# Low halves of the weights by one VectorE operation, the first casts of two items by ScalarE, and two units' scores as one TensorE task

## The chip, the cores and the metric

The kernel runs on one core of one Trainium2 chip. The metric is the device time of one execution in microseconds (us), as the median of repeated runs. Engines are named as in the profile: PE is TensorE, DVE is VectorE, ACT is ScalarE, POOL is GpSimd and SP is SyncE, whose queue issues most transfers. PEld is the loading of PE's stationary operand.

## What is computed

Block-sparse attention over 4 batches, 8 heads, 768 tokens and head size 64, followed by a two-layer network with a leaky ReLU. Everything is float32 at the interface, except that the weights of the network come as float64 in the arrays and the three random blocks of each query block as integers.

```python
scores = scale * np.matmul(q, k.transpose(0, 1, 3, 2))
# a query block of 32 sees: its neighbours (|i - j| <= 1), block 0, the last block,
# three sampled blocks; query blocks 0 and 23 see all
scores = np.where(mask, scores, -1000000000.0)
scores = scores - np.max(scores, axis=-1, keepdims=True)
attn = np.exp(scores)
attn = attn / (np.sum(attn, axis=-1, keepdims=True) + 1e-09)
x = np.matmul(attn, v)           # 3072 tokens of 512 after the heads are put side by side
h = x @ w_in                     # 512 x 2048
out = np.maximum(0.01 * h, h) @ w_out   # 2048 x 512
```

## The kernel before

**Two halves for each number.** PE multiplies float16. To keep the precision, every operand is scaled by a power of two and split into a high half, which is the value cast to float16, and a low half, which is the value minus its high half, again as float16. A product is made of three matmuls (high by high, high by low, low by high).

**Units and items.** The queries are cut in tiles T of two blocks (64 rows; tile 0 holds the first and the last block, which see all keys). A unit is one tile with one pair of heads hp; two units, hp and hp+1, make a pair. Four tiles with four head pairs each make an item of 16 units; there are 12 items, three to a batch, and so 192 units, numbered in u.n. In tiles other than 0 a unit's keys are 384: 6 fixed blocks and 6 sampled ones, which GpSimd copies out of the turned keys kt into the tile kg (line 1111) for all heads at once. Units of tile 0 have two parts of 384 keys.

**The way of a unit.** unit_scores (line 1165): four matmuls of 64 x 384 put the scores in one of the two PSUM banks s0 and s1; the left operands are half as wide as PE, and two such matmuls run side by side. unit_ttr (1189): DVE reads the scores, adds the mask em, writes p and the minimum mx. unit_exp (1200): ACT's exponential, with sums. pair_norm (1210): reciprocals r for both units of the pair. unit_high (1222): ACT makes the high half of p times r in pp. unit_split (1229): DVE makes the low half, and a transfer that transposes puts both in one of six tiles pt. pair_av (1245): twelve matmuls for each unit multiply pt with the gathered values vg into the bank av0. tile_evac (1263): ACT, DVE, ACT and POOL turn a finished tile of av0 into the two halves of x.

**The network.** For an item of 256 tokens, FF is worked off in 8 chunks. ffn_h (1285): 24 matmuls make a chunk of h in a PSUM bank. ffn_act1 (1298, ACT) and ffn_max (1303, DVE) make the leaky ReLU in ht. ffn_act2 (1308) casts it to the high half of g on DVE and subtracts on POOL for the low half. ffn_o (1313): 12 matmuls with the right-hand weights. For items 0 and 1 ("early": 2) the chunks become eligible quarter by quarter, as soon as that quarter's weights are made; later items need all of them. add_ffn (1422) queues an item's chunks "lead" (8) steps after its last unit, and refill (1434) releases them once its four tiles are evacuated (nx is 4).

**The weights.** w_in and w_out are cut in four quarters each, eight parts in the order wi0, wo0, wi1, ... wo3. Parts 0 to 5 are handled in two groups of 128 x 1024, parts 6 and 7 in four of 128 x 512. decode (813) turns the 64-bit patterns to float32 with one ACT and three DVE operations. squares (665) sums squares on PE for the scale. Then finish (864) splits each group, by the letter that "wsplit" has for the part. With "p" (parts 0 to 5 before):

```python
nc.scalar.activation(hi, g.d3, AF.Copy, scale=s[:, :1])
nc.scalar.activation(g.d, g.d, AF.Copy, scale=s[:, :1])
nc.gpsimd.tensor_tensor(out=lo, in0=g.d3, in1=hi, op=ALU.subtract)
```

With "d" (part 6 before) a single DVE scalar_tensor_tensor takes the place of the last two lines. Part 7 has a branch of its own, which is the same before and after.

**What sets the order.** The program text does not set it. Each call of an engine is recorded as a task with the memory cells that it reads and writes (class Plan, line 182; Engine, 433), and with a priority: plan.level (237) gives 1000 + 200 for each step, a step being one unit. plan.block (244) joins several PE matmuls into one task. Plan.trial (253) then plays the engines with a table of costs (466): each engine takes the ready task of lowest priority value, and PE adds a penalty (stay) for a task whose operands have another width than the last one's ("a" for half, "f" for full). Then the latest start of each task becomes its priority, and the trial is made again, up to four times, as long as the modelled end improves. The order of the best trial is issued, and each engine works through its own part of it in order.

The main loop (1575) goes through the units. In each step it takes the letters of "ord" in turn, "dtsixScmgovabphw". Those that matter here: d is pair_norm, t is unit_ttr, s is split_step, i is unit_high, x is unit_exp, S is the scores of the next unit, g is ffn_act2, a is av_step, v is one stage of tile_evac, h is ffn_h. split_step (1546) keeps count of the pt tiles in use (tlive) and calls av_step(True) where the next would exceed "pt" (6). When it has split the second unit of a pair, it puts the pair in pend_av, due "av_lag" (3) steps later; av_step (1557) takes due pairs out.

Of the kernel before, what the change touches and what calls it, by code (L numbers as in the profile page):

```python
# [34 lines left out]
    "bs": 1500,  # L35
    "kcopy": 330.0, "load": 800.0, "fetch": 1100.0, "early": 2,
    "pe_t": 16,
    "passes": 4,
    "stay_ns": 2000.0,
    "kg_dma": 0,  # L40
    "flag": 1,
    "g": 2,
    "g_at": 0,
# [20 lines left out]
    "wp": [2, 5, 14, 17, 20, 23, 26, 29],  # L64
    "wlead": 4,
    "wr": [(0, 1.0), (4, 3.0), (10, 4.0), (18, 4.5)],
    "wsplit": "ppppppdd",
    "xbufs": 3,
}

# [111 lines left out]
class Plan:  # L182
# [59 lines left out]

    @contextmanager
    def block(self, eng="PE"):
        g = Task()
        g.eng, g.run, g.busy, g.late, g.kind, g.loads, g.reads, g.writes = eng, [], 0.0, 0.0, "", [], set(), set()
        g.port = False
        self.group = g
        yield
        self.group = None  # L250
        self.add(g)
# [214 lines left out]
def cost(eng, method, a, k):  # L466

    out = k.get("out", a[0] if a else None)
    n = elements(out)
    apply = lambda x: hasattr(x, "ap")  # L470
    if eng == "PE":
        lhs, rhs = a[1], a[2]
        cols = elements(rhs)
        if lhs.dtype == F32:
            return 60.0 + 4 * cols, 300.0 + 4 * cols, "f", []
        half = elements(lhs) <= 64
        t = cols / 2.4 + 2.5
        return (t / 2 if half else t), t + 180, ("a" if half else "f"), []
    if eng == "SP" or method.startswith("dma"):
        turned = method == "dma_start_transpose"  # L480
        w = transfer(k["out"], k["in_"], turned)
        rows = len([d for d in list(k["out"].ap) if d[1] > 1])
        busy = 1050.0 + 0.37 * n if turned else 425.0 + 110 * max(0, rows - 1)
        return busy, busy, "", [w]
    if eng == "DVE":
        ptr = sum(1 for x in (k.get("scalar"), k.get("scalar1"), k.get("scale")) if apply(x)) > 0
        src = [x for m, x in k.items() if m in ("in0", "in1", "in_") and apply(x)]
        wide = [x for x in src if elements(x) > 1]
        f = 1.0
        if method in ("tensor_copy", "tensor_scalar") and len(wide) == 1 and wide[0].space == bass.MemoryType.SB:  # L490
            f = 0.5
            if method == "tensor_copy" and wide[0].dtype == F16 and out.dtype == F16:
                f = 0.25
        if method == "tensor_reduce":
            n = elements(k["in_"])
        d = 145 + 62 * ptr + n * f / 0.96
        if len(wide) == 2 and all(x.space == bass.MemoryType.SB for x in wide) and n >= 256:
            d *= 1.08
        acc = method == "tensor_tensor_reduce"
        return max(d - 70, 60.0), d + 12 + 80 * acc, "", []  # L500
    if eng == "ACT":
# [10 lines left out]
def tile_block_sparse_attention_ffn(  # L512
# [67 lines left out]
    cst, pw, sm, pa, pf = Pool(1), Pool(1), Pool(4), Pool(2), Pool(2)  # L580
    banks = [Buffer(psum.tile([P, 512], F32, name=n)) for n in ("s0", "s1", "o0", "o1", "h0", "h1", "h2", "av0")]
    group = {"s": banks[:2], "o": banks[2:4], "h": banks[4:7], "av": banks[7:]}
    turn = dict.fromkeys(group, 0)
    wide = Buffer(banks[0].ap[:, KEYS:])
    slots = [Buffer(banks[1].ap[:, at:at + 16]) for at in range(KEYS, 512, 16)]
# [102 lines left out]
    eq = tmps[:NB, 150:150 + NR * NB].rearrange("p (r b) -> p r b", r=NR)  # L688
    sels = [tmps[:NB, 222 + P * a:222 + P * (a + 1)].rearrange("p (a b c) -> p a b c", a=2, b=2) for a in range(2)]
    assert 222 + 2 * P <= DM and 6 + 2 * NB * NR <= 150  # L690
    offs = cst.tile([1, NT - 1, 8], I32, name="offs")
    vrow = cst.tile([P, 2, NT - 1], I32, name="vrow")
    lane = cst.tile([P, 2, NT - 1], I32, name="lane")
    mask = cst.tile([P, NT - 1, SLOTS], F32, name="mask")
    lane_m = cst.tile([P, NT - 1, SLOTS], F32, name="maskhalf")

    def load_constants():
        nc.sync.dma_start(out=eye, in_=c_eye)
# [101 lines left out]
    def load_w(g):  # L800
# [12 lines left out]
        def decode():  # L813


            plan.prio = 1000.0 + 200 * CFG["wp"][g.part]
            lo, hi, f, d = raw[:, :, 0], raw[:, :, 1], g.d, g.d.bitcast(I32)
            nc.scalar.activation(f, hi.bitcast(F32), AF.Copy, scale=2.0 ** -112)
            nc.vector.tensor_scalar(out=d, in0=d, scalar1=3, scalar2=None, op0=ALU.logical_shift_left)
            nc.vector.scalar_tensor_tensor(  # L820
                out=d, in0=lo, scalar=29, in1=d, op0=ALU.logical_shift_right, op1=ALU.bitwise_or)
            nc.vector.scalar_tensor_tensor(
                out=d, in0=hi, scalar=-0x80000000, in1=d, op0=ALU.bitwise_and, op1=ALU.bitwise_or)
            busy.difference_update(held)
        return decode

# [3 lines left out]
    def prep_weights():  # L830
# [33 lines left out]
        def finish(n, kind, gs):  # L864
            plan.prio = 1000.0 + 200 * CFG["wp"][gs[0].part]
            inv, s = scales(squares([g.d for g in gs], f"{kind}{n}", "w"), 1, f"{kind}{n}", keep=f"{kind}{n}", fl="w")
            invs[kind, n] = inv
            yield 1
            for i, g in enumerate(gs):
                hi, lo = g.d16[:, :, 1, :], g.d16[:, :, 0, :]  # L870
# [5 lines left out]
                    nc.vector.tensor_copy(out=hi, in_=tmp)  # L876
                else:
                    nc.scalar.activation(hi, g.d3, AF.Copy, scale=s[:, :1])
                    if CFG["wsplit"][g.part] == "p":
                        nc.scalar.activation(g.d, g.d, AF.Copy, scale=s[:, :1])  # L880
                        nc.gpsimd.tensor_tensor(out=lo, in0=g.d3, in1=hi, op=ALU.subtract)
                    else:
                        nc.vector.scalar_tensor_tensor(
                            out=lo, in0=g.d3, scalar=s[:, :1], in1=hi, op0=ALU.mult, op1=ALU.subtract)
                yield g.w
            if kind == "wo":
                pr = cst.tile([P, 1], F32, name=f"pr{n}")
                nc.vector.scalar_tensor_tensor(
                    out=pr, in0=invs["wi", n][:, :1], scalar=1.0 / GDOWN, in1=inv[:, :1], op0=ALU.mult, op1=ALU.mult)
                undo[n] = pr  # L890
                done.add(n)

# [21 lines left out]
        for n in range(NQ):  # L914
# [3 lines left out]
            nc.vector.tensor_scalar(out=g2, in0=g1, scalar1=0.01, scalar2=None, op0=ALU.mult)  # L918
            down[n] = (g1, g2)
        done.add("all")  # L920
        yield 1


# [69 lines left out]
    def prep_k(b, hp, rk):  # L993
# [32 lines left out]
        else:  # L1026
            for h in range(2):
                turned("h", kts[b][:, 2 * hp + h, :], k16.rearrange("p n l d -> p (n l d)")[:, h * S:(h + 1) * S],
                       "DVE" if h else "ACT")
        kready[b, hp] = True  # L1030
        yield 1.2

# [56 lines left out]
    def gather_k(b, T):  # L1089
# [3 lines left out]
        n = n0 % 2  # L1093
        kg = kgb[n]
        t0 = (T - 1) * Q2
        if n0 < CFG["kg_dma"]:
            nc.sync.dma_start(out=kg[:, :, :P], in_=kt[:, :, t0:t0 + P])
# [8 lines left out]
        for a in range(2):  # L1106
# [13 lines left out]
        nc.gpsimd.tensor_copy(  # L1120
            out=em.bitcast(I32).rearrange("p (n l) -> p n l", l=BLOCK // 2),
            in_=mask[:, T - 1, :].bitcast(I32).unsqueeze(2).to_broadcast([P, SLOTS, BLOCK // 2]))
        kgs[b, T] = kg, em
# [37 lines left out]
            return g  # L1161
        return wrap

    @levelled(lambda u: u.n + CFG["pr"][0])
    def unit_scores(u):
        i, c0 = u.k // 2, u.k % 2 * Q2
        require_qk(u.b, u.j, i, u.hp)
        if u.T:
            require_kg(u.b, u.T)
# [1 line left out]
        if key not in nscale:  # L1171
            score_scale(*key)
        u.nsc = nscale[key]
        qs, qxs, _ = qstack[u.b, u.j, i]
        u.sp = []
        for part in range(u.parts):
# [68 lines left out]
    def pair_av(pr):  # L1245
# [2 lines left out]
            avs[pr.item.n, pr.T] = bank(f"av_{pr.nm}", "av").rearrange("p (n l t) -> p n l t", n=NP, l=2)  # L1248
        pr.av = avs[pr.item.n, pr.T]
        for u in pr.units:  # L1250
            require_v(u.b, u.hp, u.T)
            n = NCH * u.parts
            with plan.block():
                for c in range(n):
# [52 lines left out]

    def ffn_act2(c):
        c.g = pf.tile([P, 2, 2, N2], F16, tag="g", name=f"g_{c.item.nm}_{c.f}", bufs=CFG["g"])
        nc.vector.tensor_copy(out=c.g[:, 0], in_=c.t)  # L1310
        nc.gpsimd.tensor_tensor(out=c.g[:, 1], in0=c.t, in1=c.g[:, 0], op=ALU.subtract)

    def ffn_o(c):
# [232 lines left out]
    def split_step():  # L1546
        if pend_split:
# [27 lines left out]
    for u in units:  # L1575
# [32 lines left out]
        n = int(credit)  # L1608
        credit -= n
        if step == 0:  # L1610
            unit_scores(u)
        c = aq[0] if aq else None
        for w in CFG["ord"]:
# [119 lines left out]
```

## Time and profile before

| what | us |
|---|---|
| median of 3 runs | 844.78 (842.82 to 851.21) |
| the profiled execution, its own time | 852.83 |
| its span from first to last instruction | 851.1 |
| PE busy | 750.1 |
| DVE busy | 597.5 |
| ACT busy | 502.5 |
| POOL busy | 372.3 |
| mean granted PE clock | 0.938 |

The profile is of one execution. Its page has a row for each engine with the busy tenths in 40 equal slices of the span. The other views used are: busy times by stretch of time; the waits of an engine, each put down to what ended it; groups of instructions of one engine, operation and shape, with count, busy time and mean duration; and the timeline, where neighbouring instructions of one kind are merged into a row with a count (so a row's duration can hold waits between them). Almost all instructions are recorded by one helper, so their line is L451, and the groups are told apart by the names of tiles: W for the weights, g and ht for the network's middle, s, p, pp, pt, av, vg for the attention. Where an instruction's input and output have the same tile name W, it is a step of the decoding or splitting of weights. Matmuls are pipelined: the duration of a merged row of matmuls includes the filling of the array, and the distance of two starts tells their throughput.

### The profile page before, as it was taken

The page shows a single profiled execution, that of the slowest core. Times are in us where ns is not written, and L with a number is a line of the kernel's source. Part 1 is how long each engine was busy: PE and PEld are TensorE (multiplying, and loading weights), DVE is VectorE, ACT ScalarE, POOL GpSimd, SP SyncE. Part 2 cuts the span into 40 slices and gives each one's busy share as a digit, 9 for nine tenths or more (in the row PEclk, how much of TensorE's full clock was granted, in tenths as well). Part 3 has the DMA queues.
Part 4 walks back from the last instruction along what each step waited for, and adds up shares of the span by engine and source line. Part 5 has one row for each costly group of instructions (what it writes and reads, how often), then busy time and mean ns, then how long its engine had stood idle before and what let it go on. Part 6 is the DMA issues. An engine that isn't in the chain of part 4 may idle for free. (4 is left out here: it accounts for less than half of the span.)

```text
span 851.1 us, 19895 instructions
## 1 busy us (share of the span) xinstructions
PE 750.1 (88%) x7204; PEld 492.0 (58%) x7204; DVE 597.5 (70%) x1642; ACT 502.5 (59%) x1087; POOL 372.3 (44%) x558
## 2 busy tenths in 40 slices
PE   3565656688979999999999999999999999979997
PEld 2353445455646656666665666656656666656674
DVE  5897699988768887878867577589587575662221
ACT  6779677566665665757647566476466464552111
POOL 0225457634323555554544446455435364532221
PEclk9567679689989999999999999999999999999999
DMA  9615966598797999999989989789568687591000
GB/s 189 230 39 173 331 149 196 137 192 183 136 150 165 202 206 194 173 213 179 218 163 158 204 152 214 149 160 226 127 130 174 119 157 129 104 165 25 13 14 25
DMA packets 305326, 133.28 MB, mean 157 GB/s; under 512 B 272205, under 2 KB 284621, under 8 KB 305229
## 3 DMA queue, kind: packets, MB, share of 16 engines
q1 hardware_dynamic: 299596, 114.71, 66.9%
q0 software_dynamic: 5632, 17.31, 9.5%
q8 instruction: 56, 0.92, 0.5%
q14 instruction: 42, 0.34, 0.1%
HBM read 65.65 MB, written 12.58 MB: 92 GB/s over the span
## 5 line engine op out<-in xcount | busy, mean ns | idle before, releaser
L451 PE MATMUL h<-x,W 128*128 128x256 f16 x2304 | 285.4, 280 | 8.6 <-ACT x L451 7.8
L451 PEld LDWEIGHTS <-W 128*128 128x128 f16 (+1 forms) x2480 | 240.2, 102 | 80.0 <-issue 24.3
L451 PE MATMUL o<-W,g 128*128 128x512 f16 x1152 | 272.1, 382 | 0.7 <-POOL g L451 0.7
L451 POOL TENSOR_TENSOR g<-ht,g 128x512 f16<-128x512 f32 x96 | 116.8, 1217 | 231.1 <-DVE g L451 182.3
L451 PEld LDWEIGHTS <-g 128*128 128x128 f16 x1152 | 107.4, 99 | 127.2 <-issue 16.6
L451 ACT ACTIVATE p<-p,mx 128x384 f32<-128x384 f32 x208 | 126.0, 607 | 68.8 <-DVE mx L451 66.7
L451 DVE SCALAR_TENSOR_TENSOR pp<-p,r,pp 128x384 f16<-128x384 f32 x208 | 143.4, 721 | 29.3 <-ACT pp L451 27.8
L451 ACT ACTIVATE pp<-p,r 128x384 f16<-128x384 f32 x208 | 117.6, 606 | 34.9 <-issue 11.9
L451 DVE SCALAR_TENSOR_TENSOR ht<-h,gd,ht 128x512 f32<-128x512 f32 x80 | 59.9, 748 | 94.7 <-ACT ht L451 94.3
L451 ACT ACTIVATE ht<-h,gs 128x512 f32<-128x512 f32 x80 | 54.6, 682 | 116.8 <-PE h L451 106.8
L1146 POOL DMA_INDIRECT vg<-scr,vrow x88 | 90.7, 1031 | 70.4 <-PE av L451 49.9
L451 DVE CUSTOM_DVE_ANT_0 p<-s,em,nsc 128x384 f32<-128x384 f32 x176 | 105.3, 609 | 22.7 <-PE s L451 21.5
L1111 POOL COPY kg<-kt 128x128 int32 x264 | 82.3, 348 | 69.2 <-PE s L451 55.3
L451 PE MATMUL av<-pt,vg 128*64 128x128 f16 x2112 | 83.0, 225 | 15.6 <-DMA pt<-pp 8.1
L451 PEld LDWEIGHTS <-vg 128*64 128x64 f16 x2112 | 67.2, 112 | 44.4 <-issue 33.3
L451 PE MATMUL s<-kg,qs 128*64 128x384 f16 x352 | 61.8, 346 | 9.6 <-DVE mx L451 4.2
L451 PE MATMUL s<-kg,qxs 128*64 128x384 f16 x352 | 60.8, 339 | 0.2 <-DMA qxs<-qs 0.2
L451 POOL TENSOR_TENSOR x<-xf,x 128x256 f16<-128x256 f32 x48 | 35.9, 748 | 34.3 <-ACT x L451 32.5
L451 DVE CAST g<-ht 128x512 f16<-128x512 f32 x96 | 42.8, 445 | 10.2 <-PE o L451 7.4
L451 PEld LDWEIGHTS <-qs 128*64 128x64 f16 x416 | 27.7, 113 | 34.9 <-issue 28.5
L451 ACT ACTIVATE avt<-av 128x256 f32<-128x256 f32 x48 | 18.1, 378 | 37.1 <-PE av L451 33.8
L451 ACT ACTIVATION_READ_ACCUMULATOR p<-p,mx 128x1 f32 x208 | 39.3, 189 | 0.0
(127 smaller groups left out, 765.5 us busy)
## 6 DMA issues: line engine op xcount, KB each, us to landing
vg<-scr SPq DMA_DIRECT2D x44, 256.0 KB
v<-in_v_dram SPq DMA_DIRECT2D x32, 192.0 KB
qxs<-qs SPq DMA_DIRECT2D x48, 128.0 KB
scr<-v SPq DMA_DIRECT2D x16, 384.0 KB
rq<-in_q_dram SPq DMA_DIRECT2D x20, 256.0 KB
W<-in_moe_w_in_dram SPq DMA_DIRECT2D x5, 1024.0 KB
out_dram<-ob SPq DMA_DIRECT2D x20, 256.0 KB
rk<-in_k_dram SPq DMA_DIRECT2D x24, 192.0 KB
```

The source lines that it names most:

```text
L451: self.plan.task(self.eng, lambda: f(*a, **k), busy, late, reads, writes, kind, loads, port)
L1111: tc.nc.gpsimd.tensor_copy(out=kg.ap.bitcast(I32)[:, :, slot * BLOCK // 2:(slot + 1) * BLOCK // 2], in_=kt.ap.bitcast(I32)[:, :, bass.ds(o ...
L1146: tc.nc.gpsimd.indirect_dma_start(into.ap, None, scr[b].ap, bass.IndirectOffsetOnAxis(ap=at.ap, axis=0))
```

## The change

Three things are changed in what is computed where, and a few in the details.

First, "wsplit" has "d" for all parts: in the twelve groups of parts 0 to 5 the second ACT copy and the POOL subtraction are replaced by one DVE scalar_tensor_tensor, which multiplies by the scale and subtracts the high half.

Second, "gact": for items 0 and 1 the first cast of ffn_act2 is made by ACT.

Third, PE's tasks. From unit 48 on ("pair_at"), except for tile 0, the scores of both units of a pair are recorded as one task. The values of a pair are one task everywhere. A value task that is due at that moment is to be part of the score task ("join"), and from unit 48 on a pair is due 5 steps after its split ("av_lag2"). plan.block can be nested for that, and what the scores need beforehand is moved to before_scores, the evacuation's bookkeeping to before_av and after_av.

The details: the products pr and betas are made by tensor_scalar in place of two-tensor operations; the scratch tile of the masks lies in memory that is used already; the planner's price of a float32 matmul is lower. The diff also brings branches for other settings ("e" in wsplit, "p" in sign, kg_act, em_act, kt_act), none of which is taken.

```diff
-    "wsplit": "ppppppdd",
+    "wsplit": 'dddddddd',
+    "pair_at": 48,
+    "join": 1,
+    "av_lag2": 5,
+    "gact": (0, 1),
...
     def block(self, eng="PE"):
+        if self.group is not None:
+            yield
+            return
...
         if lhs.dtype == F32:
-            return 60.0 + 4 * cols, 300.0 + 4 * cols, "f", []
+            return 60.0 + 4 * cols / 2.4, 300.0 + 4 * cols / 2.4, "f", []
...
+    lane_m = tmps[:, 222:222 + (NT - 1) * SLOTS].rearrange("p (t n) -> p t n", n=SLOTS)
...
-    lane_m = cst.tile([P, NT - 1, SLOTS], F32, name="maskhalf")
...
-                nc.vector.scalar_tensor_tensor(
-                    out=pr, in0=invs["wi", n][:, :1], scalar=1.0 / GDOWN, in1=inv[:, :1], op0=ALU.mult, op1=ALU.mult)
+                nc.vector.tensor_scalar(
+                    out=pr, in0=invs["wi", n][:, :1], scalar1=inv[:, :1], scalar2=1.0 / GDOWN,
+                    op0=ALU.mult, op1=ALU.mult)
...
-    @levelled(lambda u: u.n + CFG["pr"][0])
-    def unit_scores(u):
-        i, c0 = u.k // 2, u.k % 2 * Q2
+    def before_scores(u):
+        i = u.k // 2
         require_qk(u.b, u.j, i, u.hp)
...
+
+    @levelled(lambda u: u.n + CFG["pr"][0])
+    def unit_scores(u):
+        i, c0 = u.k // 2, u.k % 2 * Q2
...
         for u in pr.units:
-            require_v(u.b, u.hp, u.T)
...
-        nc.vector.tensor_copy(out=c.g[:, 0], in_=c.t)
+        if c.item.n in CFG["gact"]:
+            nc.scalar.activation(c.g[:, 0], c.t, AF.Copy)
+        else:
+            nc.vector.tensor_copy(out=c.g[:, 0], in_=c.t)
...
-            nc.vector.tensor_tensor(out=betas[key], in0=undo[key[1]], in1=vscale[it.b][:, :1], op=ALU.mult)
+            nc.vector.tensor_scalar(
+                out=betas[key], in0=undo[key[1]], scalar1=vscale[it.b][:, :1], scalar2=None, op0=ALU.mult)
...
-                pend_av.append((step + CFG["av_lag"], pu.pair))
+                pend_av.append((step + CFG["av_lag2" if pu.n >= CFG["pair_at"] else "av_lag"], pu.pair))
 
     def av_step(now=False):
         if pend_av and (now or pend_av[0][0] <= step):
             pr = pend_av.popleft()[1]
-            tlive[0] -= 2 * pr.units[0].parts
-            while evs and pr.hp == 0:
-                ev_step()
-            pair_av(pr)
-            if pr.hp == NP - 2:
-                vfree[0] += pr.T > 0
-                evs.append((pr.n, tile_evac(pr)))
+            before_av(pr)
+            with plan.block():
+                pair_av(pr)
+            after_av(pr)
+
+    def before_av(pr):
+        while evs and pr.hp == 0:
+            ev_step()
+        for u in pr.units:
+            require_v(u.b, u.hp, u.T)
+
+    def after_av(pr):
+        tlive[0] -= 2 * pr.units[0].parts
+        if pr.hp == NP - 2:
+            vfree[0] += pr.T > 0
+            evs.append((pr.n, tile_evac(pr)))
...
             elif w == "S" and step + 1 < len(units):
-                unit_scores(units[step + 1])
+                nu = units[step + 1]
+                if nu.n < CFG["pair_at"] or nu.T == 0:
+                    with plan.level(nu.n + CFG["pr"][0]):
+                        before_scores(nu)
+                    unit_scores(nu)
+                elif nu.pi == 0:
+                    with plan.level(nu.n + CFG["pr"][0]):
+                        for x in nu.pair.units:
+                            before_scores(x)
+                    due = CFG["join"] and pend_av and pend_av[0][0] <= step
+                    if due:
+                        before_av(pend_av[0][1])
+                    with plan.level(nu.n + CFG["pr"][0]):
+                        with plan.block():
+                            for x in nu.pair.units:
+                                unit_scores(x)
+                            if due:
+                                pair_av(pend_av[0][1])
+                    if due:
+                        after_av(pend_av.popleft()[1])
```

More of the change, by code (lines that the diff above doesn't have):

```diff
@@ L37 @@
     "pe_t": 16,
+    "pair_at": 48,
+    "join": 1,
+    "av_lag2": 5,
+    "sign": "dddddddd",
     "passes": 4,
     "stay_ns": 2000.0,
-    "kg_dma": 0,
+    "kg_act": 0,
+    "em_act": 0,
+    "gact": (0, 1),
+    "kt_act": 0,
     "flag": 1,
@@ L582, in tile_block_sparse_attention_ffn @@
     group = {"s": banks[:2], "o": banks[2:4], "h": banks[4:7], "av": banks[7:]}
+    if "e" in CFG["wsplit"]:
+        group["wl"], group["h"] = [group["h"][2]], group["h"][:2]
     turn = dict.fromkeys(group, 0)
@@ L821, in decode @@
                 out=d, in0=lo, scalar=29, in1=d, op0=ALU.logical_shift_right, op1=ALU.bitwise_or)
-            nc.vector.scalar_tensor_tensor(
-                out=d, in0=hi, scalar=-0x80000000, in1=d, op0=ALU.bitwise_and, op1=ALU.bitwise_or)
+            if CFG["sign"][g.part] == "p":
+                nc.scalar.activation(hi.bitcast(F32), hi.bitcast(F32), AF.Sign)
+                nc.gpsimd.tensor_tensor(out=f, in0=f, in1=hi.bitcast(F32), op=ALU.mult)
+            else:
+                nc.vector.scalar_tensor_tensor(
+                    out=d, in0=hi, scalar=-0x80000000, in1=d, op0=ALU.bitwise_and, op1=ALU.bitwise_or)
             busy.difference_update(held)
@@ L867, in finish @@
             invs[kind, n] = inv
+            if CFG["wsplit"][gs[0].part] == "e":
+                neg = sm.tile([P, 1], F32, tag="neg", name=f"neg_{kind}{n}", bufs=2)
+                nc.vector.tensor_scalar(out=neg, in0=s[:, :1], scalar1=-1.0, scalar2=None, op0=ALU.mult)
             yield 1
@@ L878, in finish @@
                     nc.scalar.activation(hi, g.d3, AF.Copy, scale=s[:, :1])
-                    if CFG["wsplit"][g.part] == "p":
+                    if CFG["wsplit"][g.part] == "e":
+                        if not i:
+                            dg = cst.tile([P, P], F32, tag="dg", name=f"dg_{kind}{n}")
+                            nc.scalar.activation(dg, eye, AF.Copy, scale=neg[:, :1])
+                        for c in range(g.w):
+                            pb = bank("wl", "wl")
+                            with plan.block():
+                                nc.tensor.matmul(pb, dg, g.d3[:, c, :], start=True, stop=False)
+                                nc.tensor.matmul(pb, eye16, hi[:, c, :], start=False, stop=True)
+                            nc.scalar.activation(lo[:, c, :], pb, AF.Copy, scale=-1.0)
+                    elif CFG["wsplit"][g.part] == "p":
                         nc.scalar.activation(g.d, g.d, AF.Copy, scale=s[:, :1])
@@ L887, in finish @@
                 pr = cst.tile([P, 1], F32, name=f"pr{n}")
-                nc.vector.scalar_tensor_tensor(
-                    out=pr, in0=invs["wi", n][:, :1], scalar=1.0 / GDOWN, in1=inv[:, :1], op0=ALU.mult, op1=ALU.mult)
+                nc.vector.tensor_scalar(
+                    out=pr, in0=invs["wi", n][:, :1], scalar1=inv[:, :1], scalar2=1.0 / GDOWN,
+                    op0=ALU.mult, op1=ALU.mult)
                 undo[n] = pr
@@ L920, in prep_weights @@
         done.add("all")
+        if "wl" in group:
+            group["h"].extend(group["wl"])
+            turn["h"] = 2 + turn["h"] % 2
         yield 1
@@ L1028, in prep_k @@
                 turned("h", kts[b][:, 2 * hp + h, :], k16.rearrange("p n l d -> p (n l d)")[:, h * S:(h + 1) * S],
-                       "DVE" if h else "ACT")
+                       "DVE" if h and not CFG["kt_act"] else "ACT")
         kready[b, hp] = True
@@ L1095, in gather_k @@
         t0 = (T - 1) * Q2
-        if n0 < CFG["kg_dma"]:
-            nc.sync.dma_start(out=kg[:, :, :P], in_=kt[:, :, t0:t0 + P])
+        if n0 < CFG["kg_act"]:
+            nc.scalar.activation(kg[:, :, :P], kt[:, :, t0:t0 + P], AF.Copy)
         else:
@@ L1119, in gather_k @@
         em = pa.tile([P, KEYS], BF16, tag="em", name=f"em_{b}_{T}", bufs=2)
-        nc.gpsimd.tensor_copy(
+        if n0 < CFG["em_act"]:
+            nc.scalar.activation(
+                em.rearrange("p (n l) -> p n l", l=BLOCK),
+                mask[:, T - 1, :].unsqueeze(2).to_broadcast([P, SLOTS, BLOCK]), AF.Copy)
+        else:
+          nc.gpsimd.tensor_copy(
             out=em.bitcast(I32).rearrange("p (n l) -> p n l", l=BLOCK // 2),
@@ L1309, in ffn_act2 @@
         c.g = pf.tile([P, 2, 2, N2], F16, tag="g", name=f"g_{c.item.nm}_{c.f}", bufs=CFG["g"])
-        nc.vector.tensor_copy(out=c.g[:, 0], in_=c.t)
+        if c.item.n in CFG["gact"]:
+            nc.scalar.activation(c.g[:, 0], c.t, AF.Copy)
+        else:
+            nc.vector.tensor_copy(out=c.g[:, 0], in_=c.t)
         nc.gpsimd.tensor_tensor(out=c.g[:, 1], in0=c.t, in1=c.g[:, 0], op=ALU.subtract)
@@ L1610, in tile_block_sparse_attention_ffn @@
         if step == 0:
+            before_scores(u)
             unit_scores(u)
@@ L1621, in tile_block_sparse_attention_ffn @@
             elif w == "S" and step + 1 < len(units):
-                unit_scores(units[step + 1])
+                nu = units[step + 1]
[11 more added lines that the diff above has]
+                    with plan.level(nu.n + CFG["pr"][0]):
+                        with plan.block():
+                            for x in nu.pair.units:
[4 more added lines that the diff above has]
+                        after_av(pend_av.popleft()[1])
             elif w == "t":
```

## The prediction

> **What bounds the kernel now.** I read first the page's row of slices (21.3 us each), then the busy times by stretch, then TensorE's waits, then groups and single rows. The slices:
>
> ```profile
> PE   3565656688979999999999999999999999979997
> PEld 2353445455646656666665666656656666656674
> DVE  5897699988768887878867577589587575662221
> ```
>
> PE is about half busy for eight slices and nearly full after the twelfth; DVE is the other way round. The same by stretch (length; busy us and instructions of PE, PEld, DVE, ACT, POOL; granted clock, DMA share, GB/s):
>
> ```profile
> core 0 of [0], span 851.1 us
> ...
> 0.00:250.00 250.00, 166.97 (x1552) 113.49 (x1553) 200.07 (x551) 171.29 (x327) 102.26 (x140) 0.80 0.75 175
> 250.00:750.00 500.00, 491.25 (x4948) 318.17 (x4947) 369.94 (x1035) 307.49 (x716) 247.68 (x397) 1.00 0.89 171
> ```
>
> So there are two kernels in one. Up to 250 us PE stands idle for 250 - 167 = 83 us, its clock is 0.80, and DVE, at 80%, is the fullest engine. From 250 to 750 PE is 98% busy at full clock: there only less PE time helps. What shortens the first stretch brings the second forward by as much. The largest waits of PE up to 275 us (total, times, longest):
>
> ```profile
> PE s L451 <- DVE W L451: 9.9, 3, 5.1
> PE o L451 <- ACT pp L451: 9.4, 5, 3.7
> ```
>
> No single wait rules: the decoding of the weights (W) on DVE and the probabilities (pp) on ACT lead a list of many.
>
> **The low halves.** In six of eight weight parts, two groups each, an ACT copy and a GpSimd subtraction become one DVE operation. GpSimd's groups from 40 to 205 us, where all the subtractions lie (count, busy us, mean ns):
>
> ```profile
> L451 POOL TENSOR_TENSOR W<-W 128x1024 f16<-128x1024 f32 x12 | 27.6, 2314 | 23.7 <-ACT W L451 23.3 <-POOL kg L1111 0.3
> L1146 POOL DMA_INDIRECT vg<-scr,vrow x17 | 19.0, 1118 | 17.1 <-PE av L451 12.8 <-issue 2.3 <-DMA scr<-v 1.8
> L1111 POOL COPY kg<-kt 128x128 int32 x48 | 17.4, 398 | 14.4 <-PE s L451 12.1 <-DVE kg L451 1.2 <-DVE s L451 1.1
> L451 POOL TENSOR_TENSOR g<-ht,g 128x512 f16<-128x512 f32 x6 | 7.9, 1320 | 24.7 <-DVE g L451 15.0 <-DVE r L451 9.7
> ```
>
> And the groups by shape, over the whole span, that price the rest:
>
> ```profile
> L451 DVE SCALAR_TENSOR_TENSOR pp<-p,r,pp 128x384 f16<-128x384 f32 x208 | 143.4, 721 | 29.3 <-ACT pp L451 27.8 <-issue 0.7
> ...
> L451 DVE CAST g<-ht 128x512 f16<-128x512 f32 x96 | 42.8, 445 | 10.2 <-PE o L451 7.4 <-DVE ht L451 0.5 <-issue 0.2
> ...
> L451 DVE SCALAR_TENSOR_TENSOR W<-kt,W 128x512 int32<-128x512 int32 x16 | 16.3, 1050 | 0.0
> ...
> L451 ACT ACTIVATE qa<-rq 128x512 f16<-128x512 f32 x24 | 14.9, 619 | 4.3 <-DMA qs<-qa 3.5 <-DMA qxs<-qs 0.8
> ...
> L451 DVE SCALAR_TENSOR_TENSOR k<-rk,sc_s,k 128x768 f16<-128x768 f32 x12 | 12.2, 1015 | 2.9 <-ACT k L451 2.9
> ...
> L451 ACT ACTIVATE W<-W,wi_s 128x1024 f32<-128x1024 f32 x6 | 6.6, 1133 | 0.0
> ...
> L451 DVE SCALAR_TENSOR_TENSOR W<-W,wi_s 128x512 f16<-128x512 f32 x4 | 2.8, 767 | 0.0
> ```
>
> GpSimd loses 27.6 us. ACT loses 12 copies of 1.13 us, 13.6 us (the x6 row is half of them). DVE gains 12 operations of 1024 columns: 767 ns at 512 and 1015 ns at 768 columns give 0.97 ns a column, so 1.26 us each, 15.2 us in all, on the fullest engine. That alone would be a loss. But two rows of the timeline, DVE's and GpSimd's, lie on top of each other:
>
> ```profile
> 79.70 3.26 DVE L451 SCALAR_TENSOR_TENSOR pp<-p,r,pp 128x384 f16<-128x384 f32 x2 [0.93 <-ACT pp L451]
> 80.40 2.13 POOL L451 TENSOR_TENSOR W<-W 128x1024 f16<-128x1024 f32 x1
> 82.69 1.11 POOL L1146 DMA_INDIRECT vg<-scr,vrow  x1 [0.16 <-issue]
> ```
>
> Two pp operations, 2 x 0.72 = 1.4 us by their mean, take 3.3 us when a subtraction of 2.13 us falls on them: 1.8 us more. The decode operations show it as a spread (minimum, median and maximum in ns):
>
> ```profile
> L451 DVE SCALAR_TENSOR_TENSOR W<-kt,W x22: 673/728/3726, 42.7 to 202.5; 128x512 int32<-128x512 int32 x16, 128x1024 int32<-128x1024 int32 x6
> ```
>
> The 16 of 512 columns have a mean of 1050 ns against a median of 728: 16 x 0.32 = 5.2 us lost to a few that stood. So a subtraction costs DVE nearly its own 2.1 us whenever DVE has an operation with two SBUF operands next. Bounds for the stalls that go: these two places, 7 us, and all twelve subtractions in full, 27.6 us. I take 16, about the middle: DVE is 80% busy there and most of that work has two such operands, but some stalls may have other causes. The gather at 82.69 is a second gain: it stood behind the subtraction.
>
> The Trainium skill, SBUF — State Buffer, section "SBUF: two separate sides", says that DVE and GpSimd share one port pair as an exclusive lock, which a DVE operation with two SBUF inputs takes, against a GpSimd operation that reads SBUF, for the whole instruction. The rows above agree. The rule also speaks against the change: the new operation has two such inputs and takes the lock too, so it can queue behind GpSimd's other work and hold it up. The third rival prices that from rows.
>
> **The casts.** For items 0 and 1 (16 chunks) the first cast of g goes from DVE (16 x 0.445 = 7.1 us less) to ACT (16 x 0.62 = 9.9 us more, by the qa row of this shape). ACT nets -13.6 + 9.9 = -3.7 us, so it still gains. A chunk's chain grows by 0.17 us and a change of engine; PE's other tasks cover it, and without them it would be 16 x 0.17 = 3 us.
>
> **DVE in the first stretch:** +15.2 - 7.1 - 16 = -8 us. PE there waits for DVE and ACT in turn, so I carry it over one for one: **-8 us**. Ends: 15.2 + 5 (half the third rival's waits) - 7.1 - 7 = +6, and 15.2 - 7.1 - 27.6 = -19.
>
> **The PE tasks.** From unit 48 on, two units' scores are one task, and everywhere a pair's two value products are one. What leaving the half-width operands costs, in the full stretch, between the first and the last such excursion from 250 to 750 us:
>
> ```profile
> 251.85 0.85 PE L451 MATMUL av<-pt,vg 128*64 128x128 f16 x12
> ...
> 502.29 0.33 PE L451 MATMUL s<-kg,qs 128*64 128x384 f16 x2
> 502.45 0.33 PE L451 MATMUL s<-kg,qxs 128*64 128x384 f16 x2
> 502.71 1.48 PE L451 MATMUL h<-x,W 128*128 128x256 f16 x12
> ...
> 747.86 0.53 PE L451 MATMUL av<-pt,vg 128*64 128x128 f16 x12
> ```
>
> A score couple takes 502.45 - 502.29 = 0.16 us, so the last one's turn is over at 502.61; h starts at 502.71, 0.10 us later. I take as much for the way in: 0.2 us an excursion. Counted on the PE timeline there are 111, 22 us, for some 70 pairs: the order made before already joins much. After it, 66 pairs have two tasks each, scores and values, that may meet in one excursion: between 66 and 132. I take 95, near the middle: **-3 us**, ends -9 and +4.
>
> The code also means to join a due value task to the scores. It will hardly ever do so: a unit is split three steps after its own, so a pair that ends with unit n falls due at n + 3 + 5 = n + 8; in that step the split stands ahead of the scores in the order string, six pt tiles are then alive, a seventh exceeds the limit of 6, and the value task goes out alone. It also goes out two steps later than before, and an item's FFN with it. Data and buffers depend as before and the planner reorders by latest starts, so I cost this at nothing; the cover is PE's stock of FFN tasks. Without it two steps of (851 - 250) / 144 = 4.2 us would stand open at each of ten items. No DMA is added or moved past another in a queue but with its value task.
>
> The small operations (pr, betas), the mask's half tile and the planner's price of an f32 matmul: a few instructions, 0, ends -1 and +1.
>
> **Sum.** -8 - 3 = -11 us. The profiled execution took 852.8 us (span 851.1 and 1.7 around it), the median of the runs shown is 844.8; so 842 for a run like the profiled one and **834 us** for the median.
>
> **Rivals.** First, the gain reaches further (chance 0.2): stalls go at nearly all twelve subtractions (25 us, so -17 on DVE) and scores meet values in most pairs (-9): -26, 819 us. For it speaks that pp's mean holds stalls all through; against it, that PE's early waits have many owners.
>
> Second, only the tasks gain (0.14): the first stretch is a chain of ACT, DVE and transfers, and the freed time turns into idling: -3, 842 us. For it speak the scattered waits; against it, DVE's 80%.
>
> Third, the port stays taken (0.10): the new operations wait for GpSimd's six g of 1.32 us and six of its kg copies of 0.40 us, 10 us, which eats most of the relief: DVE nets +2, with -3 from the tasks 844 us. This is the lock of the skill's page turned on the change. Against it: the subtractions were the longest holders by far.
>
> Fourth, slower (0.12): a joined score task needs both score banks, so it can't start until DVE has read the second unit too, where a single one needed only the first. One read, and what PE waited for these reads from 275 to 760 us:
>
> ```profile
> L451 DVE CUSTOM_DVE_ANT_0 p<-s,em,nsc 128x384 f32<-128x384 f32 x176 | 105.3, 609 | 22.7 <-PE s L451 21.5 <-issue 0.5
> ```
>
> ```profile
> PE s L451 <- DVE mx L451: 3.4, 3, 1.5
> ```
>
> Uncovered at all 66 joined tasks, 0.61 us is 40 us. From 18 tasks on (11 us) it eats the gain; at 50 it gives 834 + 30 = 864 us. Against it: only 3.4 us of such waiting so far, and twelve matmuls of an FFN task (1.48 us above) cover one read.
>
> That the joining of values does nothing is settled above and part of the forecast.
>
> **How the numbers follow.** Forecast 0.44, rivals 0.2, 0.14, 0.10, 0.12. About 1% (8.4 us) is what a measurement of this kernel can tell from no change; the three runs shown spread by as much. Faster than 836.3: 0.44 x 0.7 + 0.2 + 0.14 x 0.2 = 0.54. Slower than 853.2: 0.12 x 0.8 + 0.10 x 0.3 = 0.13. The rest, 0.33, is within 1%. The range runs from a little below the first rival to beyond the third, with the mild part of the fourth: 817 to 852; the forecast's own is 826 to 842.
>
> **What would show it.** Right: no GpSimd rows of W; twelve DVE rows of W with 128x1024 and f16 out near 1.26 us; pp's mean well under 721 ns and no decode operation near 3.7 us; PE idle before 250 us down from 83 to about 75; 80 casts of g on DVE; fewer than 111 excursions. Wrong: DVE no less busy before 250 us; p or mx rising among PE's waits after it; PE idle from 250 to 750 us well above 500 - 491 = 9 us.

## The result and the profile after

The changed kernel takes 820.4 us as the median of 4 runs (820.2 to 824.5), the kernel before in the same session 843.8 us. The ratio is 0.9717, with a 95% interval of 0.9651 to 0.9783. It is faster, by 23 us; 11 were forecast. The profiled execution took 820.6 us, with a span of 818.5.

The slices of the changed kernel's page, 20.5 us each:

```profile
PE   3466576688999999999999999999999999999997
PEld 3245454456567666757665666666666766767664
DVE  5797789889979877977877687678786766754121
```

PE is now full from the eleventh slice, and the gap near the end is gone. The two traces are best set side by side at the same work, and not at the same time. I cut them within the 48th of the 208 score tasks (the last one ahead of unit 44, near the end of batch 0, about where PE becomes the bound) and within the 192nd (the last one ahead of unit 176, the first of the last item). First the kernel before, then the changed one, with the columns as in the prediction:

```profile
0.00:229.89 229.89, 151.34 (x1416) 104.44 (x1418) 186.79 (x505) 159.84 (x303) 96.20 (x133) 0.79 0.72 178
229.89:711.42 481.53, 468.43 (x4711) 301.43 (x4707) 357.84 (x1010) 299.16 (x693) 233.24 (x369) 0.99 0.92 174
711.42:851.10 139.68, 130.31 (x1085) 86.18 (x1080) 52.86 (x127) 43.53 (x92) 42.85 (x57) 0.99 0.31 62
```

```profile
0.00:217.75 217.75, 145.81 (x1392) 103.12 (x1394) 182.69 (x515) 151.57 (x297) 69.65 (x120) 0.78 0.77 188
217.75:689.55 471.80, 463.88 (x4728) 313.65 (x4724) 361.76 (x997) 304.59 (x702) 230.13 (x371) 1.00 0.91 178
689.55:818.50 128.95, 122.61 (x1092) 83.21 (x1086) 52.76 (x127) 44.10 (x93) 41.32 (x56) 1.00 0.29 65
```

All three parts are shorter: the first by 12 us, the middle by 10, the last by 11. (That is 33 us, because the profiled execution before was 9 us over its median of 843.8; the shares are good to some us only.) PE idle falls from 78.5 to 71.9 in the first part, from 13.1 to 7.9 in the middle and from 9.4 to 6.3 in the last.

The last two parts are best read together, for the cut splits PE's work a little differently. In the last part the changed kernel has 24 h and 18 o matmuls fewer and 47 av matmuls more; at 0.109, 0.216 and 0.03 us from start to start that is about 5 of the 11 us, work that it has already done in the middle. The kernel before also has a hole there, in which PE stands at a value task whose transposed transfer hasn't landed, and behind it matmuls that are slower than the same ones elsewhere:

```profile
760.81 0.33 PE L451 MATMUL s<-kg,qxs 128*64 128x384 f16 x2
764.89 0.53 PE L451 MATMUL av<-pt,vg 128*64 128x128 f16 x12 [3.75 <-DMA pt<-pp]
765.35 2.33 PE L451 MATMUL o<-W,g 128*128 128x512 f16 x6
767.47 3.64 PE L451 MATMUL h<-x,W 128*128 128x256 f16 x24
```

From 765.8 to 769.2 us the granted clock was 0.50, and so it was from 247.0 to 253.8 us. The changed kernel's clock is 1.00 from its first cut to 818 us. Half the clock for 10.2 us costs PE about 5 us (an estimate, half of that time). So from unit 44 on the profile of before is some 20 us longer, mostly by three things: 8 us of idling, 5 us of clock and 8 us of excursions to half-width operands, which are shown below.

The rows that answer to those of the prediction:

```profile
L461 DVE SCALAR_TENSOR_TENSOR pp<-p,r,pp 128x384 f16<-128x384 f32 x208 | 134.6, 676 | 25.9 <-ACT pp L461 24.8 <-DMA qxs<-qs 0.4
...
L461 DVE CAST g<-ht 128x512 f16<-128x512 f32 x80 | 35.5, 444 | 8.5 <-PE o L461 6.8
...
L461 DVE SCALAR_TENSOR_TENSOR W<-kt,W 128x512 int32<-128x512 int32 x16 | 11.2, 744 | 0.0
...
L461 ACT ACTIVATE g<-ht 128x512 f16<-128x512 f32 x16 | 10.0, 623 | 5.4 <-DVE ht L461 4.6 <-DVE v_i L461 0.8
...
L461 DVE SCALAR_TENSOR_TENSOR W<-W,wo_s 128x1024 f16<-128x1024 f32 x6 | 8.4, 1419 | 0.0
...
L461 DVE SCALAR_TENSOR_TENSOR W<-W,wi_s 128x1024 f16<-128x1024 f32 x6 | 7.5, 1276 | 1.2 <-ACT W L461 1.2
```

The twelve new operations take 1.28 and 1.42 us. The decode operations of 512 columns are down at 744 ns from 1050, and pp at 676 from 721. There is no GpSimd row of W left. On PE there are 72 excursions to half width between 250 and 750 us, where there were 111; from unit 44 on they are 40 fewer. A stretch of the PE timeline shows what one looks like now:

```profile
499.83 2.78 PE L461 MATMUL h<-x,W 128*128 128x256 f16 x24
502.54 0.35 PE L461 MATMUL s<-kg,qs 128*64 128x384 f16 x2
502.73 0.33 PE L461 MATMUL s<-kg,qxs 128*64 128x384 f16 x2
502.89 0.33 PE L461 MATMUL s<-kg,qs 128*64 128x384 f16 x2
503.05 0.33 PE L461 MATMUL s<-kg,qxs 128*64 128x384 f16 x2
503.21 0.84 PE L461 MATMUL av<-pt,vg 128*64 128x128 f16 x24
503.98 1.47 PE L461 MATMUL o<-W,g 128*128 128x512 f16 x6
```

Two units' scores, then both value products of an earlier pair, then full width again. The way in costs 0.09 us here: from the start of h to the first score are 2.71 us, where 24 h matmuls followed by o take 2.62 (513.48 to 516.10 us). So the prediction's 0.2 us for an excursion holds. Of the 70 excursions in the middle part, 32 have just this form. The joining in the program text isn't what does it: with "join" off, every engine has the same instructions in the same order. The planner puts the two tasks next to each other by itself.

### The profile page after: what moved, and what is told of

Its sections match the earlier page's. It is cut to its first block, busy times and chain, and to the rows that moved or that the text cites. A ratio compares the mean times of both kernels' runs of the same rounds, so it can differ in the third digit from the quotient of the medians.

```text
span 818.5 us, 19856 instructions
## 1 busy us (share of the span) xinstructions
PE 732.3 (89%) x7204; PEld 500.0 (61%) x7204; DVE 597.2 (73%) x1638; ACT 500.3 (61%) x1091; POOL 341.1 (42%) x546
## 5 line engine op out<-in xcount | busy, mean ns | idle before, releaser
L461 PE MATMUL h<-x,W 128*128 128x256 f16 x2304 | 273.8, 275 | 4.8 <-DVE ht L461 2.4
L461 PEld LDWEIGHTS <-W 128*128 128x128 f16 (+1 forms) x2480 | 237.8, 101 | 64.7 <-issue 15.7
L461 PE MATMUL o<-W,g 128*128 128x512 f16 x1152 | 265.7, 379 | 3.2 <-DVE ob L461 1.7
L461 PEld LDWEIGHTS <-g 128*128 128x128 f16 x1152 | 110.3, 99 | 122.3 <-issue 4.3
L461 DVE SCALAR_TENSOR_TENSOR pp<-p,r,pp 128x384 f16<-128x384 f32 x208 | 134.6, 676 | 25.9 <-ACT pp L461 24.8
L461 ACT ACTIVATE pp<-p,r 128x384 f16<-128x384 f32 x208 | 117.4, 605 | 43.4 <-DVE r L461 15.2
L461 PE MATMUL av<-pt,vg 128*64 128x128 f16 x2112 | 75.9, 225 | 4.8 <-DMA vg<-scr,vrow 1.8
L461 PEld LDWEIGHTS <-vg 128*64 128x64 f16 x2112 | 70.1, 114 | 14.4 <-issue 4.7
L461 DVE CAST g<-ht 128x512 f16<-128x512 f32 x80 | 35.5, 444 | 8.5 <-PE o L461 6.8
```

What stands on the lines that cost most here:

```text
L461: self.plan.task(self.eng, lambda: f(*a, **k), busy, late, reads, writes, kind, loads, port)
```

## The experiments

Any edit makes the planner reorder everything, so two kinds of control were run. In two kernels the order of every engine was kept, and only the operations of the low halves were exchanged in their places. In two others no operation was changed, only the order, by a small change of a price. All were timed against the kernel before on the chip that they ran on; ratios are compared, since its median differed between sessions (843.8 to 851.8 us). This table holds all of them: the three parts as above, PE idle in the last two of them, and excursions from 250 to 750 us, each from one profiled execution.

| kernel | ratio to before (95%) | first | middle | last | PE idle from unit 44 | excursions |
|---|---|---|---|---|---|---|
| before | 1 | 229.9 | 481.5 | 139.7 | 22.5 | 111 |
| changed | 0.9717 (0.9651 to 0.9783) | 217.8 | 471.8 | 129.0 | 14.3 | 72 |
| changed, again | 0.9706 (0.9627 to 0.9784) | 221.7 | 471.4 | 129.0 | 13.7 | 73 |
| changed, other order | 0.9654 (0.9580 to 0.9728) | 219.4 | 469.3 | 130.6 | 12.2 | 70 |
| before, other order | 0.9925 (0.9881 to 0.9968) | 220.6 | 484.4 | 137.2 | 22.8 | 100 |
| before's order, new low halves | 0.9937 (0.9898 to 0.9976) | 222.7 | 476.1 | 140.2 | 19.1 | 109 |
| changed order, old low halves | 0.9895 (0.9833 to 0.9956) | 234.6 | 472.0 | 129.2 | 14.5 | 74 |
| before + new low halves | 0.9789 (0.9730 to 0.9847) | 217.5 | 472.9 | 139.9 | 14.8 | 105 |
| changed, old low halves | 0.9734 (0.9676 to 0.9793) | 225.5 | 469.4 | 129.5 | 10.6 | 78 |
| changed, old casts | 0.9770 (0.9703 to 0.9837) | 225.0 | 473.7 | 129.4 | 15.5 | 79 |
| changed, old low halves and casts | 0.9829 (0.9751 to 0.9907) | 231.8 | 474.8 | 129.3 | 14.9 | 81 |
| changed, single scores, lag 3 | 0.9770 (0.9713 to 0.9827) | 221.0 | 468.5 | 139.4 | 19.8 | 69 |
| changed, single values | 0.9763 (0.9683 to 0.9843) | 215.2 | 482.8 | 133.2 | 20.1 | 95 |
| changed, lag 3 | 0.9899 (0.9867 to 0.9932) | 223.9 | 482.2 | 134.5 | 25.8 | 74 |

**The theory and its rivals.** Mine was the prediction's: DVE's stalls behind the GpSimd subtractions make the first part shorter, fewer excursions the rest. Rivals: the PE tasks do nearly all; or the planner's new order does, by luck.

**The operations alone, in the order of before.**

```diff
-nc.scalar.activation(g.d, g.d, AF.Copy, scale=s[:, :1])
-nc.gpsimd.tensor_tensor(out=lo, in0=g.d3, in1=hi, op=ALU.subtract)
+nc.vector.scalar_tensor_tensor(out=lo, in0=g.d3, scalar=s[:, :1], in1=hi, op0=ALU.mult, op1=ALU.subtract)
```

The tasks are planned as before; only when they are issued, the first issues nothing and the second issues the DVE operation.

> The kernel of before with every engine's order kept, in which the ACT copy is left out and the GpSimd subtraction is replaced, at its place, by the one DVE operation. Port theory: stalls of DVE go (its mean of pp falls below 700 ns, no decode operation above 2.5 us), time 836 to 840 instead of 844 us. Order theory: within 3 us of 844. If DVE's load decides (15 us more on the fullest engine), 850 or more.

Measured 0.9937, 5 us, as the theory of the stalls had it. No DVE operation takes longer than 2.4 us now, where six did before, up to 3.7. The engines' totals of this kernel:

```profile
PE 746.7 (89%) x7204; PEld 490.4 (58%) x7204; DVE 593.3 (71%) x1654; ACT 490.3 (58%) x1075; POOL 350.5 (42%) x546
```

DVE got 15.6 us of new operations and is 4.2 us less busy than the 597.5 before. Its mean of pp is 694 ns. So its other operations got 19.8 us shorter: that is what the twelve subtractions had cost it, in the same order (the twelve ACT copies went with them; no run takes out one alone). The relief outweighs the load on DVE, and this gain isn't owed to a new order. It is 5 us of the 23, or 2 to 9 by its interval.

**The operations alone, in the order of the changed kernel**, the same exchange the other way round (the minus and plus lines above change places, for parts 0 to 5):

> The changed kernel with every engine's order kept as planned, in which each of the twelve new DVE operations is replaced, at its place, by the ACT copy and the GpSimd subtraction of before. If the port stalls are what the low halves gain (the prediction's -8 us, of which 16 us of stalls), DVE operations of 3 us and longer come back before 200 us and the time rises from 820 to 826 to 832 us. If the gain lies in the new order alone, it stays within 3 us of 820.

Measured 0.9895, 16 us over the changed kernel (0.9706, the second time): more than either theory gave. One DVE operation of 3.0 us is back, at 115 us. Totals, and what DVE waited for most in the first part; below them the same line of waits in the changed kernel, second run:

```profile
PE 735.6 (88%) x7204; PEld 501.3 (60%) x7204; DVE 594.6 (71%) x1626; ACT 512.9 (61%) x1103; POOL 367.4 (44%) x558
```

```profile
DVE W L461 <- ACT W L461: 12.2, 7, 4.4
```

```profile
DVE W L461 <- ACT W L461: 5.5, 7, 2.7
```

Without the new operations (15.9 us) DVE should fall from 596.2 us, its total in the second run, to 580.3; it has 594.6. So 14 us of stalls are back. But DVE is not busier than in the changed kernel, and still the first part is 13 to 17 us longer. Some of the time is in DVE's idling: the decode operations wait 12.2 us for ACT where they waited 5.5, probably since ACT's first decode step now stands behind some of the extra copies of 1.1 us. An order made for one set of operations can be a bad one for the other; how much of the 16 us is ACT's copies and how much GpSimd's lateness, these runs do not separate.

**The changed kernel again**, as the reference of its session:

> The changed kernel itself, again, as the reference for the others on the same chip: 0.966 to 0.978 of the kernel before.

Measured 0.9706.

**The low halves undone, planned anew:**

```diff
-    "wsplit": 'dddddddd',
+    "wsplit": "ppppppdd",
```

> The changed kernel with the setting for the low halves as before, planned anew. By the prediction's terms the -8 us of the first stretch comes back: 828 us, the scores of unit 48 about 8 to 12 us later, excursions from 250 to 750 us still near 72. If the tasks carry everything: 820 to 823 us.

Measured 0.9734: 1 to 7 us over the three ratios of the changed kernel, within the interval of the first two. Of 843.8 us that is 821, in the range that was named for the tasks carrying everything; most of the 8 us did not come back. With an order of its own, the old split loses little.

**The casts undone, and both undone**, so that only the PE tasks and the small details stay changed (the second with the line above as well):

```diff
-    "gact": (0, 1),
+    "gact": (),
```

> The changed kernel with the sixteen first casts on DVE again, planned anew. Prediction: DVE gets 7 us more in the first stretch, so 5 to 7 us over the changed kernel, ratio to before 0.977 to 0.98. If the order's scatter hides it: within 0.965 to 0.976.

> The changed kernel with low halves and casts as before: only the PE tasks and the small details are changed, planned anew. If the tasks carry most (as undoing the low halves alone suggests), it stays within 5 us of the changed kernel, ratio to before near 0.977. By the prediction's sum (-8 for the first stretch, -3 for the tasks) it would be at 0.996.

Measured 0.9770 and 0.9829. Over the mean of the three ratios of the changed kernel, 0.9692, undoing the low halves costs 0.4%, undoing the casts 0.8%, undoing both 1.4%. By these figures the PE tasks with what hangs on them give some 1.7%, 14 us, and the two other edits 1.4%, 12 us. Each of the figures holds a new order too, which by the controls below is worth up to 0.7%, 6 us, so they are rough. In both of these kernels most of the loss lies in the first part (225.0 and 231.8 us), and 2 to 5 us in the middle.

**The low halves alone, added to the kernel before:**

```diff
-    "wsplit": "ppppppdd",
+    "wsplit": "dddddddd",
```

> The kernel before with the low halves by DVE in all parts and nothing else changed, planned anew. Prediction's term for the stalls and the load, without the casts: about -1 us to -6 us, ratio 0.993 to 0.999. In the fixed order the same operations gave 0.994. If the low halves are the main cause of the gain: 0.98 or less.

Measured 0.9789, where the term forecast 0.993 or more, and a little better than what was named for the low halves as the main cause. But the first part gives 12 us and the middle another 9, where nothing of weights is done. There PE idles 5.2 us in place of 13.1, and the clock of the middle is 1.00. The next control says how to read that.

**The same operations in another order**, for the kernel before and for the changed one:

```diff
-    "fly": 1250,
+    "fly": 1260,
```

> A control: the kernel before with one price of the planner, the flight of a transfer, raised from 1250 to 1260 ns. No instruction differs, only the order. If orders as such move the time little, the ratio to before is within 0.995 to 1.005. If the planner's luck is the rival cause of the gain, it is off by 1% or more, either way.

> A control: the changed kernel with one price of the planner, the flight of a transfer, raised from 1250 to 1260 ns. No instruction differs, only the order. The same edit moved the kernel before by 0.7%. If the planner's luck is of that size here too, the ratio to before lies anywhere from 0.963 to 0.978; if the changed kernel's order is a lucky one, at the upper end or above.

Measured 0.9925 and 0.9654. The kernel before gains 0.7% from nothing but an order; the changed one isn't the luckier of its two. So a single replanned comparison is uncertain by something like 0.7% beside its interval, and the order that was before was the poorer of the two tried. The luck of the order can be part of the gain, but not most of it: against the other order of before, the changed kernel is still 2% faster. What the low halves alone are worth stays open: 2.1% added to before, 1.4% against its other order, 0.4% taken from the changed kernel. Only the 5 us in the fixed order are free of this.

**Single scores:**

```diff
-    "pair_at": 48,
+    "pair_at": 1000,
```

> The changed kernel with single score tasks throughout and the lag of 3 that goes with them (a pair's values stay one task), planned anew. If the tasks gain by fewer excursions, they rise from 72 to 90 or 110 between 250 and 750 us and the time by 0.2 us for each, to 824 to 828 us. If the low halves carry everything: 820 to 822 us.

The time came out as expected, 0.9770, and the reason didn't: there are 69 excursions, no more than with joined scores. What is longer is the last part, 139.4 against 129.0 us. Its busy times, in pieces of 20 us:

```profile
750.00:770.00 20.00, 20.00 (x128) 12.25 (x125) 4.71 (x8) 3.05 (x5) 4.61 (x4) 1.00 0.01 1
770.00:790.00 20.00, 13.49 (x171) 10.83 (x170) 4.93 (x11) 5.35 (x11) 2.62 (x3) 0.83 0.18 48
```

PE has worked off its FFN tasks, takes the last scores only at 770 us, and then idles 6.5 us through the way of the last units. In the changed kernel the last scores come at 743 us, with FFN tasks left to fill the way. All kernels with single scores have a last part of 137 to 140 us; those with joined scores and a lag of 5 have 129 to 133; with joined scores and a lag of 3 (below) it is 134.5. But they don't share one reason: in the kernel before, FFN tasks stand behind the last scores as well (24 h, 12 o and again 24 h from 774.4 us), PE idles only 4.5 us after the last scores, and its last part is longer by the work that lies in it, the hole and the clock.

**Single values**, each of a pair's two products a task again, with the joined scores kept:

```diff
             before_av(pr)
-            with plan.block():
-                pair_av(pr)
+            pair_av(pr)
             after_av(pr)
```

> The changed kernel in which the two value products of a pair are two tasks again, each with the priority of its own unit, planned anew; scores stay joined. If the value tasks are what cut the excursions (with single scores there were still 69 of them), they rise to about 90 to 110 between 250 and 750 us and the time by 0.2 us for each, 4 to 8 us over the changed kernel. If the joined scores do it, excursions stay near 72 and the time within 2 us.

Measured 0.9763, 6 us over the changed kernel on the same chip, with 95 excursions. 22 more than its 73, at 0.2 us, are 4.4 us: the excursions go with the value tasks. PE's idling rises too, from 13.7 to 20.1 us, so the time can't be put down to the excursions alone.

**A joining that takes place:** with a lag of 3 a pair falls due before the limit of six pt tiles is reached.

```diff
-    "av_lag2": 5,
+    "av_lag2": 3,
```

> The changed kernel with a lag of 3 in place of 5 for the values. With 5 the pt limit takes the value task out one letter before the scores, so that it is never joined (setting the joining off gives the same order on every engine). With 3 a pair falls due at step n + 6, ahead of the limit, and the joining does work. If it is worth anything, excursions from 250 to 750 us fall from 72 towards 66 and the time by about 1 us or, since scores then wait for transposed transfers, rises by some us: ratio 0.965 to 0.985.

Measured 0.9899, 16 us slower than the changed kernel, with 74 excursions: nothing is saved. PE's largest waits from 250 us on, here and in the changed kernel's second run:

```profile
PE s L461 <- DVE mx L461: 4.0, 4, 2.0
PE h L461 <- POOL x L461: 2.7, 2, 2.3
PE s L461 <- DVE r L461: 2.7, 4, 0.8
PE av L461 <- DVE xf L461: 2.2, 3, 0.9
```

```profile
PE s L461 <- DVE mx L461: 2.4, 3, 0.9
PE s L461 <- DVE r L461: 1.5, 3, 0.9
PE h L461 <- ACT x L461: 1.4, 1, 1.4
```

PE idles 25.8 us from unit 44 on where it idled 13.7. Lag and joining were changed together here, so which of them costs it stays open; that the lag of 5 with the joining idle is the better of the two settings is shown.

## Why the prediction was right in direction and half in size

The place of the gain was right: a first part ruled by DVE, ACT and waits, and a PE-bound rest. The measured 820 us lies at the first rival's 819, but that is partly luck: of the first rival's two terms the excursions came and the 25 us of stalls did not, and idling, clock and order, which it didn't have, made up the rest.

**The stalls, 16 us forecast: confirmed in size.** With the order kept, exchanging the operations moved 19.8 us of stalls in one order and 14 us in the other. In the changed kernel as planned, the total of DVE is 597.2 against 597.5 us, so with 15.9 us of new operations and 7.3 us of casts less, 8.9 us of stalls are gone net. Other operations got longer, the copies kg from 518 to 641 ns. That isn't the low halves' doing: with the old ones kg takes 643 ns in the changed order and 611 with the tasks alone, and with the new ones 514 in the order of before. A new order by itself moves the total of DVE as well (592.7 us in the other order of before). **The third rival** did not come: the twelve new operations took 15.9 us, 0.7 more than the forecast 15.2, where that rival had them wait 10 us.

**"I carry it over one for one": right in sum, by a wrong reckoning.** The forecast for low halves and casts was -8 us; undoing both costs 12 us (0.9829 against 0.9692, with the luck of an order in it), and the mean first part of the five kernels with old low halves is 228.5 us, of the nine with new ones 220.5; the other order of before, with 220.6, is among the five. But DVE's busy time in the first part fell only from 186.8 to 182.7 us, and before 250 us it rose from 200 to 210, which the prediction had named as a sign against it. The first part isn't as long as DVE's work; the kernel with DVE least busy in it (179.1 us, the changed order with old low halves) has the longest one. So DVE's busy time is not what sets its length. That the sequence of ACT, DVE and GpSimd does, in which an ACT copy and a late subtraction go as well, fits the waits but was not tested. The forecast left ACT's 3.7 us out of the sum.

**"I take 95, near the middle: -3 us": the term that was mis-sized.** There are 72, near the lower end of 66, so 39 less at 0.2 us, 8 us. The prediction's edge of -9 covered that. It had counted on scores and values meeting in half of the pairs; the planner lets them meet in most. The value products as one task do this (95 excursions without it), and the joined scores don't (69 without them).

**"The cover is PE's stock of FFN tasks", costed at nothing: the term that is missing.** No run shows a cost of the longer lag. But the sum had no term for PE's idling and clock after the first stretch, and there the profiles differ by 8 us of idling (22.5 against 14.3 from unit 44 on) and some 5 us of clock. The prediction saw no stall to be removed there, though the row of slices shows one: the 7 near the end is the hole of 3.75 us. Which edit removes the idling stays open. With joined scores, the value tasks and the lag of 5 it is 10.6 to 15.5 us, and undoing one or two of the three gives 19.8 to 25.8; yet the new low halves alone, added to before, have 14.8. And as the profiled execution of before was 9 us over its median, part of this may be that execution's own.

**The joining that doesn't join** was right, and so was that it costs nothing. **The slower rival**, score tasks that wait for both banks, did not come: PE's waits for mx from 250 us on are 2.4 us in the changed kernel's second run. **The rival that only the tasks gain** did not come either: in the fixed order of before the new low halves alone gave 5 us.

**Left out:** the planner's luck. Of 23 us some 6 may be the poor order of before, by the one control that was run.

## What to carry to other kernels

Where a planner orders everything, an edit's gain is the operation's own price plus a new order: run the same program with a harmlessly changed price, and the exchanged operation in the old order, before believing half a per cent. Adding an operation to a full DVE can pay if it removes a GpSimd operation that stops it: here 15.6 us of new work took away 19.8 us of stalls. When tasks on the bounding engine are regrouped, look at its idling all along and at the end: in the kernel with single scores the last scores came after all the FFN work, with nothing left to hide behind. And where two parts of two traces are compared, count the work in them first.

## What the runs showed of the hardware

In the two fixed orders twelve GpSimd subtractions of 2.3 us, with the ACT copies that go with them, cost DVE 14 to 20 us, 1.2 to 1.7 us each, without appearing in any list of waits: the time is inside the DVE operations' own durations. Even operations on one column show it. The four betas took 1013 ns each in the mean in the kernel before, and 175 ns in the same order with the subtractions replaced:

```profile
L451 DVE TENSOR_TENSOR beta<-pr,v_i 128x1 f32<-128x1 f32 x4 | 4.1, 1013 | 0.0
```

```profile
L451 DVE TENSOR_TENSOR beta<-pr,v_i 128x1 f32<-128x1 f32 x4 | 0.7, 175 | 0.0
```

The mean comes from two of the four, of 1626 and 2017 ns, which lie on subtractions; the other two took 265 and 144. The first one, and GpSimd beside it:

```profile
60.38 1.63 DVE L451 TENSOR_TENSOR beta<-pr,v_i 128x1 f32<-128x1 f32 x1
```

```profile
57.78 4.21 POOL L451 TENSOR_TENSOR W<-W 128x1024 f16<-128x1024 f32 x2 [22.86 <-ACT W L451]
```

Both end at 62.0 us. The change also made the betas a product with a scalar read from a tensor, at 206 ns each. That form is not what made them shorter: the old one takes less where no subtraction lies beside it.
